# The folded query weight built in the output weight's room, two low parts of the value weight on GpSimd, and all queues in a new order

## The chip, the cores and the metric

The kernel runs on one core of a Trainium2 chip. A core has five instruction queues that run side by side and wait for one another by semaphores: TensorE (PE in the profile, its weight loads apart as PEld), VectorE (DVE), ScalarE (ACT), GpSimd (POOL) and SyncE (SP), which in this kernel issues all transfers. The metric is the device time of one execution in microseconds (us).

## The reference

Two layer types alternate, twice over, on 2048 rows of 512 numbers in float32. Both see the same weights each time.

```
x = x + A(layernorm(x))    # linear attention with a learned feature map
x = x + B(layernorm(x))    # relu(x @ w1) @ w2, inner width 1792
x = x + A(layernorm(x))
x = x + B(layernorm(x))

A(x): q, k, v = split(x @ wqkv)               # 32 heads of 16
      pq, pk = q @ w_phi, k @ w_phi           # per head
      phi = concat(softmax(p), softmax(-p))   # 32 features per head
      kv, z = sum_s phi_k v, sum_s phi_k
      o = (phi_q kv) / (phi_q z + 1e-6);  return o @ wo
```

Since `w_phi` follows `wqkv` with nothing between them, the kernel multiplies the key part and the query part of `wqkv` by `w_phi` once, at the start. It calls this folding.

## The kernel before

**Numbers in two halves.** Every float32 operand of a large product is scaled by a power of two and split into a float16 high part and a float16 low part, and a product is three matmuls: high by high, high by low, low by high (`PAIRS`, line 625). `split` (lines 417 to 431) makes the two parts of a weight: ScalarE writes the high part (line 419) and VectorE the low part as weight times scale minus high part (line 429). With `pool=True` ScalarE scales the weight in place as well and GpSimd subtracts (line 426).

**Tiles and stages.** The rows are taken in 16 blocks of 128 (`NCH`), in the feed-forward part in 8 tiles of 256 (`NT`). The front stage (lines 1635 to 1783) loads and prepares the weights and, block by block, normalises, makes keys and values (`keys`, `values`: 12 matmuls each, line 635) and sums them into a per-head table (`gather`). `opening` (line 1841) turns that table into a right-hand side, reads out the first queries, projects them with `wo` and normalises for the first feed-forward tile. Then `tile_steps` runs the feed-forward part, mixed with attention work of other blocks, and the whole is done once more for the second pair of layers.

**Folding.** `fold` (lines 1655 to 1706) takes a 512x512 weight in float32, `src`. For each of four column groups g, TensorE transposes four 128x128 blocks into a PSUM bank (line 1665, tile `wt_q`), and the bank is copied to SBUF (line 1670, tile `wT_q`). TensorE then multiplies the transposed weight by the block-diagonal `bd` made from `w_phi`, once for each of four row blocks k (line 1701, tile `pf_q`), and `split` makes the folded weight's parts `wq_h` and `wq_l` from that PSUM bank. The scale of the split comes from the sum of squares of the weight: ScalarE squares it (line 372, into the room of the low part as scratch), TensorE sums over partitions (line 382, tile `sb_q`), VectorE bounds it (line 387), GpSimd takes the power -1/2 (line 391), VectorE cuts it to a power of two (line 392). The four banks `wt_q` and the bank of `sb_q` and the four `pf_q` all come from the tag `h`, which has two banks: the third transposition needs the first copy done, the fourth the second copy, `sb_q` the third copy, the first `pf_q` the fourth.

**Rooms.** The 8 KB per partition pieces that hold a raw weight, or a transposed one, come from a pool with three rooms (`piece`, line 501). They are used by `st_k`, `st_v`, `wT_k`, `st_q`, `w1_last`, `wT_q`, `w2_last` and `wo_a`, made in this order; from the fourth on, each takes the room of one whose readers are done, and its first writer waits for the last of them. The parts of the folded and split weights have rooms of their own, four tiles of two (`Wq, Wk, Wv, Wo`, line 350). `Wo` is written by `wo_job` (line 1738), late in the front stage.

**What sets the order.** The program is a list of tasks with what each reads, writes and makes (`Plan.add`). `ORDER` (line 56) holds one string per queue; each digit says how many of the queue's remaining tasks, in the list's order, are passed over to find the next one (`Plan.queue`, line 213). The queues run in exactly that order, and each task waits for what it depends on. So a task that waits holds up all behind it in its queue.

The lines that the change touches:

Of the kernel before, what the change touches and what calls it, by code (L numbers as in the profile page):

```python
# [9 lines left out]
F32 = mybir.dt.float32  # L10
# [8 lines left out]
P = 128  # L19
# [35 lines left out]
DIGITS = "0123456789abcdefghijklmnopqrstuvwxyzABCDEFGHIJKLMNOPQRSTUVWXYZ"  # L55
ORDER = {
    PE:
        "000024222323210022000990837066622803359530620371010832920201713Q006310K3040G602E0810Az1y81420t0s0rr52061"
        "0m161i2hh0g30eh01fc0b0aaaaaaa01006605500001016050000105d0000000a00a4022001260000120304202030020214046621"
        "673005830133022111000001111006000000300000000000000000580000c00008e000gj00000000000000000000001111122222"  # L60
        "2222223022201111111222333333302222200000000011122011044a0e0000000000060000b00000111111110000000001110000"
        "000010300000000000000000500600c0bh00000000000b0000000000000011122222022222222222022222222222333444440333"
        "333333333334445555555577777788888999aa09008888899999999999aa09080060555044403333333302220000000000000000"
        "00000000111100100000011111122222022222222222333333333333337770666666055908888002240331100000060000006b00"
        "0000000000000001111111111000k0mjl001gg0f0e010b0aaaaagga090cddd010908077700504744403344361703111100330201"
        "1220666004450438000555044555aaaaaaaaaaaaaaaaaaabbbccccccccdddee0dd30b00990070055144033330201111111110000"
        "00001000000e0000000008000000008000000000d0G0000000000z0000000000I00000000000000000000000o00000000000l000"
        "000000000000000000e000000000000000t00000rK0000000000D0000000000000000000000p0000000000000000000000000000"
        "000800A000000000000000000l000000y00000000000000n00000000000000000000b00000000000000000000003000000000000"
        "000000f00000000a0000p0r000000000000000000000000b00000000000000000000003000000000000000000000000000000000"  # L70
        "00000000000000000000000000000000000000000000000000000000000000000000000000000000000000000000000000000000"
        "0000000000000000000000000000000003000",
    DVE:
        "33033020i110f333122132111gl16014039d042304b00h007300b00e0YdX0g00Te044e4d6f60I0c034c40A39j02h201h1g10000e"
        "j0dg77eh060e04130222220f1000440673001l10jk12h21f11111a112212117l162i21321b91a81pbo11a221pi00m22k20400000"
        "00001051706024363500570645045140883712201a0080700411311113001063500615660650368070404802001311a291171010"
        "0012245222002220110334402260500309081002420aa11006013131111312174004772066151006052000908556113122012226"
        "77167625772684706d1cc0i10ggg00e0011a119000607066337232043131200200022413080711117363107836a8837060060003"
        "502320062520330104400f4e100122116000004034030100000003360201200k0100g00000bb0091020c1b403300500hh0311d10"
        "11u51s00010v30tl232p252MM40aJ09OO20M076Za0Z904Z70400112223Z72000Z3133Zx10XZu1310Zq155f21310b11Zo1000cZj1"  # L80
        "009111ZJ1ZIZb071610ZB411ZI0441ZE101d1d10Zw1k002h36050402200292002520022520023f3010200082h300052422002521"
        "70250103221330322102a20082120e05322200620177022400200022211002200230005232200220022102210220021102120044"
        "2221020102200220301000010013100",
    ACT:
        "31201104220a02100ccbc5a30m07c7j0a150d202ai0h12mm4c2b5200Zq20jj0030Zim2l722Zc5g20ll37qq061e18c5411mm2020p"
        "4214l010Bn405k1000112051f2e112iGi01002ii0120u70100102m010u602012d31110iic800e9d6c907504499400600aa49020d"
        "db0g038100559g700440ia1083010a39050004635400051006006033494073601121033a308222502223011050030350300b1044"
        "4012000250120101174615b122021111030022061141033340100037111200020120620237201403903262340322201611130001"
        "1812a052103222014586705993074640445953830615908888447066bbc0fgb0f0ieh00ff0iie24f22a2bd2ca202806644a49447"
        "490577343308270325b51082226607565514660033325264003391088333026001300041061001100055200643021004043020gg"  # L90
        "0007102903100400e8800a6990510e531032203101460500f610c908900708074n06y6k650505e537m8lK4005G58U07C707Zq77M"
        "05K056Zh644544Zb0344Zn33001ZUZi44002Zd03111ZIj00030ZC22244401113f332ZD2130Zz2ZZa01002Zt2352030201000222Z"
        "NZZ50116055h0ZV10524457270050e020130201030Zd22260502310130330270055000524b031304003P30113022611022210504"
        "21021023321060524035103311704103301400206003022005042000002020000524030520322004040320400201030220030200"
        "00220000221140022004003321130220410220130220133010000",
    POOL:
        "10030574006a05079000960A06801v90046070b6008a00809e0070d0911180001010062522010a199407010445044130e0222208"
        "b0dfa0bcc080e7007250302000112100000220172151700506134021111310410000113022010350444300136134131200001100"
        "10440001706252112111700000020102b22288242043204030200000ddd11bb119c999a180807060413312033024440333004100"
        "1004102010000000000000011104030000066000001000010a09100020c0009cc0kk00tt007TT06001X10101S11Zj101Zgb33022"  # L100
        "222b022100Z9900Z60201101510020Zl4030232a40302211c2144130Z720121121O2112104030220330211120044406302204111"
        "m2011100024201333011311042336022250000000000002230133301111550444444423332222011100000331011111100000110",
    SP:
        "20001000201406086207z8b082a7b7cq8ud66eg055ef60151g255e44m171ao051g01e1g5121341077g004fl0h5d100it08210n44"
        "81g413h253200h0803057i3d3643n5401444408270007p050845ac62c3a340144g43e2016622649d1e45453b517al772514201bt"
        "662161956569bdq36337857651918401726aeg581dd125003b01a180a92c1cbc7a1a186a161w778a5681b0318884364d50v45q90"
        "86r1074j71025GF2t32B34c52e5k169200nu100za01c10a60808y24c0Cg50K913cb2090JbbSg8c84j98SZ447464m48947894l056"
        "714542Nb3120044002449652402a260511706301544142205751106622665012260511555141333041333000200",
}


# [164 lines left out]
def tile_kernel(ctx: ExitStack, tc: tile.TileContext, x_in, wqkv, w_phi, wo, w1, w2, out):  # L276
# [137 lines left out]
        src = inv if b is not None else a  # L414
        add(DVE, 0.15, lambda: nc.vector.reciprocal(inv.ap, src.ap), reads=[src], writes=[inv])

    def split(w, s, hi, lo, cols, reads, res, key, psum=False, pool=False):

        add(ACT, 0.16 + cols / 1160, lambda: nc.scalar.activation(hi(), w(), AF.Copy, scale=s.ap),
            reads=[*reads, s], writes=[(res, f"h{key}")])  # L420
# [8 lines left out]
        add(DVE, 0.12 + cols / 940, lambda: nc.vector.scalar_tensor_tensor(  # L429
            lo(), w(), s.ap, hi(), op0=ALU.mult, op1=ALU.subtract),  # L430
            reads=[*reads, s, (res, f"h{key}")], writes=[(res, f"l{key}")], lock=not psum)
# [1220 lines left out]
                   [(b, i if cuts > 1 else None)], [(W, f"l{k}") for k in range(KC)[ks]])  # L1652
        return sq

    def fold(src, W, name, t_banks, f_banks, copies, cuts=1):

        sq = squares_of(src, W, name, cuts)
        wT = piece(f"wT_{name}")
        pts = {}

        def blocks(i, g):
# [3 lines left out]
                nc.tensor.transpose(pts[g].ap[:, k * P:(k + 1) * P], f32_piece(src)[:, k, g * P:(g + 1) * P], ident)  # L1665

        def copy(g):
            if g == 0:
                wT.ap = wT.make()
            (nc.scalar.copy if copies[g] == ACT else nc.vector.tensor_copy)(f32_piece(wT)[:, g, :], pts[g].ap)  # L1670

        def turned(i, g, after=()):
            if i == 0:
# [3 lines left out]

        def copied(g):
            add(copies[g], 0.475 if copies[g] == ACT else 0.608, partial(copy, g), reads=[pts[g]],
                makes=[(wT, g)] if g == 0 else [], writes=[] if g == 0 else [(wT, g)])  # L1680

        if cuts > 1:
            for g in range(4):
# [11 lines left out]
        for k in range(KC):  # L1695
            pf = bank(f_banks[k], f"pf_{name}{k}")

            def products(k=k, pf=pf):
                pf.ap = pf.make()
                for g in range(4):  # L1700
                    nc.tensor.matmul(pf.ap[:, g * P:(g + 1) * P], f32_piece(wT)[:, g, k * P:(k + 1) * P],  # L1701
                                     bd.ap[:, g, :], start=True, stop=True)

            add(PE, 0.96, products, reads=[wT, bd], makes=[pf])
# [56 lines left out]
    for c in range(NCH):  # L1761
# [247 lines left out]
```

## Time and profile before

| | |
|---|---|
| three executions | 966.74, 967.08, 967.94 us; median 967.08 |
| the profiled execution | 966.96 us; span from first to last instruction 965.2 us |
| TensorE busy | 950.8 us of the span |
| VectorE, GpSimd, ScalarE busy | 694.2, 642.4, 571.1 us |
| granted TensorE clock | 1.000 |

The profile is one execution on the chip. A row of the timeline has the start, the duration, the engine, the line of the kernel, the operation, the tile written and the tiles read, the shape, and how many instructions the row joins; in square brackets the idle time of the engine before it, and what ended that. Matmuls are pipelined: one starts while the one before still runs, so the distance of the starts tells what a matmul costs TensorE. The windows view gives each engine's busy time in a stretch.

### The profile page before, as it was taken

What the parts mean: (1) busy time and instruction counts of PE and PEld (TensorE: products, weight loads), DVE (VectorE), ACT (ScalarE), POOL (GpSimd) and SP (SyncE); (2) the same over time, 40 slices, a digit from 0 to 9 for tenths busy, and PEclk for the clock granted to TensorE, in tenths of its full rate; (3) what the DMA queues carried; (4) which work ended last, traced back from release to release, by engine and by line L of the source; (5) the groups of instructions that cost most, each with busy time, mean ns of one, the idle gap of its engine ahead of it and who ended that gap; (6) DMA issues with size and microseconds to landing.
All of it is one profiled execution on the core that took longest, in us unless ns stands there. A gap on an engine that the chain in (4) does not pass through costs nothing.

```text
span 965.2 us, 24114 instructions
## 1 busy us (share of the span) xinstructions
PE 950.8 (99%) x9620; PEld 665.1 (69%) x9620; DVE 694.2 (72%) x1388; ACT 571.1 (59%) x1121; POOL 642.4 (67%) x630
## 2 busy tenths in 40 slices
PE   7999998999999999999999999999999999999998
PEld 5555554766565666667667875566667888898997
DVE  6889889974867768765485668987886665664454
ACT  7889978654454645455365564565546665555543
POOL 2598886678584866647367746268568787877563
PEclk9999999999999999999999999999999999999999
DMA  9367738577869587886938853799999886886542
GB/s 336 113 178 204 231 110 236 115 170 172 242 158 240 146 208 220 211 197 183 237 108 203 289 163 105 240 243 223 215 232 202 251 175 149 222 180 149 138 133 77
DMA packets 251809, 183.41 MB, mean 190 GB/s; under 512 B 180656, under 2 KB 188080, under 8 KB 251696
## 3 DMA queue, kind: packets, MB, share of 16 engines
q1 hardware_dynamic: 251696, 181.87, 72.3%
q8 instruction: 75, 1.23, 0.5%
q14 instruction: 38, 0.31, 0.1%
HBM read 108.30 MB, written 30.15 MB: 143 GB/s over the span
## 4 chain that ended last, share of the span: by engine, by line
PE 91%; DVE 4%; ACT 2%; DMA 1%; POOL 1%; issue 1%; SPq 0%; DVEq 0%; ACTq 0%; POOLq 0%
PE ph L1367 24%; PE py L1483 15%; PE py L1542 12%; PE pk L635 8%; PE pv L635 8%; PE pw L635 8%; PE pq L635 7%; PE ph L1447 4%; PE pn L953 2%; PE kv L803 2%; DMA xe<-in_A_x_dram 1%; DMA pT<-p_q 1%; POOL p_q L710 0%; DVE e_q L672 0%; PE pf_q L1701 0%
## 5 line engine op out<-in xcount | busy, mean ns | idle before, releaser
L1483 PE MATMUL py<-w,h 128*128 128x512 f16 x690 | 174.4, 379 | 0.0
L1367 PEld LDWEIGHTS <-s 128*128 128x128 f16 x2352 | 152.1, 98 | 30.8 <-issue 2.3
L1380 ACT ACTIVATE sn<-ph 128x128 f32<-128x128 f32 x294 | 80.3, 273 | 140.2 <-PE ph L1367 139.1
L635 PEld LDWEIGHTS <-xT 128*128 128x128 f16 x900 | 86.8, 98 | 98.8 <-issue 0.5
L1367 PEld LDWEIGHTS <-w 128*128 128x128 f16 x1764 | 111.1, 98 | 13.5 <-issue 0.2
L1367 PE MATMUL ph<-yT,s 128*128 128x128 f16 x1176 | 97.6, 219 | 1.4 <-DVE ph L1386 1.4
L1367 PE MATMUL ph<-yT,w 128*128 128x128 f16 x1176 | 97.6, 219 | 0.0
L1386 DVE TENSOR_TENSOR ph<-ph,sn 128x128 f32<-128x128 f32 x98 | 29.3, 299 | 92.9 <-PE ph L1367 54.0
L1483 PEld LDWEIGHTS <-h 128*128 128x128 f16 x690 | 61.4, 98 | 48.1
L699 POOL TENSOR_TENSOR e_q<-e_q,fm_q 128x1024 f32<-128x1024 f32 x32 | 64.0, 2000 | 39.6 <-ACT fm_q L695 39.5
L699 POOL TENSOR_TENSOR e_k<-e_k,fm_k 128x1024 f32<-128x1024 f32 x30 | 60.1, 2003 | 39.5 <-ACT fm_k L695 39.1
L710 POOL TENSOR_TENSOR p_q<-e_q,p_q 128x1024 f16<-128x1024 f32 x32 | 69.8, 2180 | 19.9 <-ACT p_q L706 19.8
L635 PE MATMUL pk<-wk_h,xT 128*128 128x512 f16 x256 | 81.3, 379 | 0.1
L635 PE MATMUL pv<-wv_h,xT 128*128 128x512 f16 x256 | 81.2, 379 | 0.0
L635 PE MATMUL pw<-wo_h,oT 128*128 128x512 f16 x256 | 81.2, 379 | 0.0
L710 POOL TENSOR_TENSOR p_k<-e_k,p_k 128x1024 f16<-128x1024 f32 x30 | 66.2, 2208 | 21.9 <-ACT p_k L706 21.6
L1391 DVE TENSOR_TENSOR ph<-ph,sn 128x256 f32<-128x256 f32 x98 | 41.9, 427 | 32.9 <-PE ph L1367 31.9
L635 PEld LDWEIGHTS <-oT 128*128 128x128 f16 x384 | 36.8, 98 | 40.2
L1542 PEld LDWEIGHTS <-h 128*128 128x128 f16 x648 | 59.2, 98 | 6.4
L1163 POOL TENSOR_TENSOR w<-r 128x256 f32<-128x256 f32 x41 | 32.2, 787 | 39.9 <-ACT r L1159 35.8
L635 PE MATMUL pq<-wq_h,xq 128*128 128x512 f16 x168 | 57.4, 379 | 0.0
L1159 ACT ACTIVATE r<-ph 128x512 f32<-128x512 f32 x54 | 32.0, 593 | 36.8 <-DVE ph L1391 36.5
(267 smaller groups left out, 2434.3 us busy)
## 6 DMA issues: line engine op xcount, KB each, us to landing
s<-s_dram SPq DMA_DIRECT2D x98, 512.0 KB, 4.5
q_dram<-qs SPq DMA_DIRECT2D x28, 256.0 KB, 2.9
ql<-q_dram SPq DMA_DIRECT2D x28, 256.0 KB, 3.7
u<-t_dram SPq DMA_DIRECT2D x13, 512.0 KB, 4.7
xt_dram<-xT SPq DMA_DIRECT2D x21, 256.0 KB, 4.8
xq<-xt_dram SPq DMA_DIRECT2D x21, 256.0 KB, 3.8
xe<-in_A_x_dram SPq DMA_DIRECT2D x16, 256.0 KB, 5.2
x<-in_A_x_dram SPq DMA_DIRECT2D x16, 256.0 KB, 3.9
```

What stands on the lines that cost most here:

```text
L635: nc.tensor.matmul(pm.ap, xT.ap[:, a, k, :], W.ap[b][:, k, :], start=(k == 0 and i == 0), stop=(k == KC - 1 and i == 2))
L699: (nc.vector if fast else nc.gpsimd).tensor_tensor(e3, e3, sm.unsqueeze(2).to_broadcast([P, 2 * n, DH]), op=ALU.mult)
L710: (nc.vector if fast else nc.gpsimd).tensor_sub(p16.ap[:, 1, cols], ef, p16.ap[:, 0, cols])
L1159: nc.scalar.activation(r.ap, ph.ap, AF.Relu)
L1163: nc.gpsimd.tensor_sub(rf.ap[:, :2, :], r.ap.rearrange("p (a b) -> p a b", a=4)[:, ::3, :], block(1).unsqueeze(1).to_broadcast([P, 2, P]))
L1367: nc.tensor.matmul(at(r), weight_of(i, b, kk, s, summed), rows_of(y, i, a, kk), start=(first and kk == 0 and n == 0), stop=(kk == 1 and n ...
L1380: nc.scalar.activation(saved(i), at(2), AF.Copy)
L1386: add(DVE, 0.27, lambda: nc.vector.tensor_tensor(at(3), at(1), saved(2), op=ALU.add), reads=[(ph, 1), (sn, 2)], writes=[(ph, 3)], boost=10 ...
L1391: add(DVE, 0.40, lambda: nc.vector.tensor_tensor(wide(ph), wide(ph), wide(sn), op=ALU.add), reads=[(sn, 0), (sn, 1)], writes=[(ph, 0), (ph ...
L1447: nc.tensor.matmul(at()[:, j, cs.start * P:cs.stop * P], W1.at(b, k, slice(f * P, (f + 1) * P)), yT.ap[:, cs, a, k, :], stop=(k == KC - 1 ...
L1483: nc.tensor.matmul(py.ap, h[a].ap.rearrange("p j t -> p (j t)")[:, cols], W2.at(b, fs[j], slice(0, D)), start=(begins and j == k == 0), st ...
L1542: nc.tensor.matmul(py.ap[:, 256 * r:256 * r + 256], left[a], right[b], start=(s == 0 and r == 0 and k == 0), stop=(last and k == 2), skip_ ...
```

## The change

Three things are changed.

1. `fold` can be given a `home`. For the query weight it is `Wo`: the transposed query weight is written, as float32, over the two part tiles of the output weight (two column groups in each), and no `piece` is made for it. The pieces are then seven: `st_k`, `st_v`, `wT_k`, `st_q`, `w1_last`, `w2_last`, `wo_a`.
2. `split` can be called with `aside`. For row blocks 2 and 3 of the value weight ScalarE makes the high part as before; GpSimd multiplies the raw weight by its scale in place and then subtracts the high part. VectorE's two instructions for these blocks go. The split of the value weight now marks the blocks of `st_v` one by one.
3. All five strings of `ORDER` are new.

```diff
-    def split(w, s, hi, lo, cols, reads, res, key, psum=False, pool=False):
+    def split(w, s, hi, lo, cols, reads, res, key, psum=False, pool=False, aside=False):
 
         add(ACT, 0.16 + cols / 1160, lambda: nc.scalar.activation(hi(), w(), AF.Copy, scale=s.ap),
             reads=[*reads, s], writes=[(res, f"h{key}")])
+        if aside:
+            add(POOL, 0.14 + cols / 700, lambda: nc.gpsimd.tensor_scalar(w(), w(), s.ap, None, op0=ALU.mult),
+                reads=[s], writes=reads)
+            add(POOL, 0.14 + cols / 523, lambda: nc.gpsimd.tensor_sub(lo(), w(), hi()),
+                reads=[*reads, (res, f"h{key}")], writes=[(res, f"l{key}")])
+            return
...
-    def fold(src, W, name, t_banks, f_banks, copies, cuts=1):
+    def fold(src, W, name, t_banks, f_banks, copies, cuts=1, home=None):
...
-        wT = piece(f"wT_{name}")
+        wT = piece(f"wT_{name}") if home is None else home
+        row = lambda g: f32_piece(wT)[:, g, :] if home is None else \
+            flat(home.ap[g // 2]).bitcast(F32)[:, g % 2 * 512:g % 2 * 512 + 512]
...
-            (nc.scalar.copy if copies[g] == ACT else nc.vector.tensor_copy)(f32_piece(wT)[:, g, :], pts[g].ap)
+            (nc.scalar.copy if copies[g] == ACT else nc.vector.tensor_copy)(row(g), pts[g].ap)
...
-                    nc.tensor.matmul(pf.ap[:, g * P:(g + 1) * P], f32_piece(wT)[:, g, k * P:(k + 1) * P],
+                    nc.tensor.matmul(pf.ap[:, g * P:(g + 1) * P], row(g)[:, k * P:(k + 1) * P],
...
     for k in range(KC):
         split(lambda k=k: f32_piece(st_v)[:, k, :], s_v, lambda k=k: Wv.ap[0][:, k, :],
-              lambda k=k: Wv.ap[1][:, k, :], 512, [st_v], Wv, k)
+              lambda k=k: Wv.ap[1][:, k, :], 512, [(st_v, k)], Wv, k, aside=k > 1)
...
-            fold(st_q, Wq, "q", "h" * 4, "h" * KC, (ACT,) * 4)
+            fold(st_q, Wq, "q", "h" * 4, "h" * KC, (ACT,) * 4, home=Wo)
```

The strings, read by the rule of line 213, give these queues in the stretch that the first two parts touch (k0 is the key product of block 0, x1 block 1 of the rows; "wT copy 0" is line 1670 for column group 0):

| queue | before | after |
|---|---|---|
| PE | sum v, wt_q 0, wt_q 1, **k0, wt_q 2**, x1 transposed, wt_q 3, **v0, sum q, pf_q 0, pf_q 1**, k1 | sum v, wt_q 0, wt_q 1, **wt_q 2, k0**, x1 transposed, wt_q 3, **sum q, pf_q 0, pf_q 1, v0**, k1 |
| ACT | wk_h 2, 3, 0, **x1 normalised, wk_h 1**, wv_h 2, 1, 0, 3, wT copy 0, 1, square of q, wT copy 3, x1 high, wT copy 2 | wk_h 2, 3, 0, **wk_h 1, x1 normalised**, wT copy 0, 1, wv_h 1, 3, 2, square of q, wT copy 2, 3, wv_h 0, x1 high |
| DVE | **statistics of x1, scale of k, x0 low**, wk_l 2, 3, 0, 1, **wv_l 2, 1, 0, 3**, k0 bounds, statistics of x2, x3 | **scale of k, x0 low, statistics of x1**, wk_l 2, 3, 0, 1, **wv_l 1**, k0 bounds, statistics of x2, bound of q, **wv_l 0** |
| POOL | power for v, for x2, x3, for q | power for v, **wv 3 multiplied, wv_l 3, wv 2 multiplied, wv_l 2**, for q, for x2, x3 |
| SP | x2, x3, w1 part 0, 2, x4, w1 part 1, x5, w1 last, x6 | x2, x3, x4, x5, w1 part 1, w1 last, w2 part 0, x6, w1 part 0 |

Over the whole program, counted among the tasks that both kernels have, 604 of 1493 tasks of PE stand at another place in their queue than before, 529 of 948 of DVE, 743 of 1071 of ACT, 347 of 618 of POOL and 426 of 506 of SP, in the mean by 0.8, 1.1, 1.6, 1.1 and 4.8 places.

More of the change, by code (lines that the diff above doesn't have):

```diff
@@ new lines @@
+    POOL:
+        "10070220044607009040960068070y016v0804607005908a0080900c700c911107001010062522010a194077a00074002022302b"
+        "22d0fh07md09ci00a008772034021103110400330017115100013633402111110111000014102220035504430013134112220000"
+        "111110033028070252222121151000020102222526455503050002010100ddd11bb1a199a9a18088000140222203302033333300"
+        "11201022300110000000000000201104030000066000001001000aa01000010b109cc0kk00tt91U0T7000411V020SZl0f000Zg41"
+        "302011c1020110Z99100Z50111000400Zn01030201219021121110238302220Z4210200N11100400201133301112155003302011"
+        "411n1011110002232033301411114130201121411211111000522244002111004444442333022111111111141444130222221000"
+        "0110",
@@ new lines @@
+    SP:
+        "2000100026912490c0egi0x8iaj450700542c33inan0342k808327v312161600314ec14b5c1a000279f10jg01120k81811q1b1j4"
+        "5314j24n323c2qa11471844d74a854915i13393v172822b787ce86e47b497772i62399552s8861a2df5674d2673864504g4117b7"
+        "12161957669b023a407717533380bb73833aegg3114c0041c1b34c48a220bcbc71080756013304544263248847740344459a99r0"
+        "a014p4135q6J3d3Gd535d00zn4141517x2d21g121x18bF711092a053b0Ba1d0Ic1cNbXe0jbpc6dc9V9a95575Z0nc14813697001U"
+        "145f24211100h4030352h4604412260003305526670132208551006622051322015141044444030244440200200",
@@ L1667, in copy @@
         def copy(g):
-            if g == 0:
+            if g == 0 and home is None:
                 wT.ap = wT.make()
-            (nc.scalar.copy if copies[g] == ACT else nc.vector.tensor_copy)(f32_piece(wT)[:, g, :], pts[g].ap)
+            (nc.scalar.copy if copies[g] == ACT else nc.vector.tensor_copy)(row(g), pts[g].ap)
         def turned(i, g, after=()):
@@ L1679, in copied @@
             add(copies[g], 0.475 if copies[g] == ACT else 0.608, partial(copy, g), reads=[pts[g]],
-                makes=[(wT, g)] if g == 0 else [], writes=[] if g == 0 else [(wT, g)])
+                makes=[(wT, g)] if g == 0 and home is None else [],
+                writes=[] if g == 0 and home is None else [(wT, g)])
         if cuts > 1:
```

81 lines of the change are left out of this document (35 added, 46 removed).

## The prediction

> **What bounds the kernel now.** I read the busy page first, then the chain that ended last, then the windows, then TensorE's waits, and the timeline only where TensorE stands still. The page:
>
> ```profile
> span 965.2 us, 24114 instructions
> PE 950.8 (99%) x9620; PEld 665.1 (69%) x9620; DVE 694.2 (72%) x1388; ACT 571.1 (59%) x1121; POOL 642.4 (67%) x630
> PEclk9999999999999999999999999999999999999999
> PE 91%; DVE 4%; ACT 2%; DMA 1%; POOL 1%; issue 1%; SPq 0%; DVEq 0%; ACTq 0%; POOLq 0%
> ```
>
> TensorE works 950.8 of 965.2 us at the full granted clock in every slice, and the chain that ended last is 91% its own. The change adds no matmul and removes none: it can only move the 965.2 - 950.8 = 14.4 us in which TensorE is idle. The windows view cuts the span where that idleness changes; its columns are the stretch and its length, then busy time of PE, PEld, DVE, ACT, POOL, clock, DMA share and GB/s:
>
> ```profile
> 0.00:26.31 26.31, 21.11 (x140) 15.75 (x141) 17.49 (x53) 19.89 (x32) 6.29 (x20) 1.00 0.93 340
> 26.31:153.00 126.69, 126.69 (x934) 65.93 (x932) 112.91 (x204) 112.08 (x170) 97.11 (x63) 1.00 0.59 168
> 153.00:168.05 15.05, 12.12 (x101) 6.60 (x100) 13.09 (x29) 11.96 (x17) 12.02 (x8) 1.00 0.80 230
> 168.05:952.00 783.95, 782.51 (x8373) 570.11 (x8372) 542.87 (x1091) 424.46 (x900) 524.00 (x538) 1.00 0.75 190
> 952.00:965.20 13.20, 8.40 (x79) 6.69 (x76) 7.87 (x15) 2.71 (x6) 2.96 (x4) 0.97 0.11 41
> ```
>
> The idle time is 5.20 us before the key product of block 1 (26.31), nothing in the rest of the front, 2.93 in the opening, 1.44 in 784 us of feed-forward work, and 4.80 in the end. The waits view names what it was for (total, times, longest):
>
> ```profile
> PE wt_q L1665 <- ACT wT_q L1670: 1.6, 1, 1.6
> PE ph L1367 <- DVE ph L1386: 1.4, 5, 0.5
> PE tr_b L578 <- ACT xn_b L612: 1.1, 1, 1.1
> PE pn L953 <- DMA pT<-p_q: 0.5, 1, 0.5
> PE tr_o L578 <- DVE dn L961: 0.4, 1, 0.4
> PE tr_o L578 <- DVE o L964: 0.3, 1, 0.3
> ```
>
> Only the first, 1.6 us, lies in the code that the first two parts of the change touch.
>
> **That stall.** Times in these rows: start, duration.
>
> ```profile
> 12.72 0.68 DVE L587 TENSOR_TENSOR xT<-tr_a,xT 128x512 f16<-128x512 f32 x1
> 12.89 1.84 ACT L419 ACTIVATE wk_h<-pf_k,s_k 128x512 f16<-128x512 f32 x3 [0.16 <-DVE s_k L402]
> 13.54 1.13 PE L1701 MATMUL pf_k<-bd,wT_k 128*128 128x128 f32 x8 [0.48 <-DVE stat_a L617]
> 14.62 0.82 ACT L612 ACTIVATE xn_a<-xe,stat_a 128x512 f32<-128x512 f32 x1
> 15.32 0.69 ACT L419 ACTIVATE wk_h<-pf_k,s_k 128x512 f16<-128x512 f32 x1
> 15.80 0.38 PE L635 MATMUL pk<-wk_h,xT 128*128 128x512 f16 x1
> 16.12 2.56 ACT L419 ACTIVATE wv_h<-st_v,s_v 128x512 f16<-128x512 f32 x4
> 16.88 2.74 DVE L429 SCALAR_TENSOR_TENSOR wv_l<-st_v,s_v,wv_h 128x512 f16<-128x512 f32 x4
> 18.36 0.38 PE L635 MATMUL pk<-wk_h,xT 128*128 128x512 f16 x1
> 19.71 1.07 ACT L1670 COPY wT_q<-wt_q 128x512 f32<-128x512 f32 x2 [1.02 <-DVE wv_l L429]
> 20.35 0.66 PE L1665 MATMUL wt_q<-ident,st_q 128*128 128x128 f32 x4 [1.61 <-ACT wT_q L1670]
> 20.67 1.92 ACT L372 ACTIVATE wq_l<-st_q 128x2048 bf16<-128x2048 f32 x1
> 20.84 0.60 PE L578 MATMUL tr_a<-ident,xn_a 128*128 128x128 f32 x4
> 21.28 0.60 PE L1665 MATMUL wt_q<-ident,st_q 128*128 128x128 f32 x4
> 21.71 0.38 PE L635 MATMUL pv<-wv_h,xT 128*128 128x512 f16 x1
> 24.30 0.28 PE L382 MATMUL sb_q<-sq_q,ones 128*128 128x1 f32 x2
> 24.44 2.03 PE L1701 MATMUL pf_q<-bd,wT_q 128*128 128x128 f32 x16
> 26.31 0.38 PE L635 MATMUL pk<-wk_h,xT 128*128 128x512 f16 x1
> ```
>
> VectorE's last low part of the value weight ends at 16.88 + 2.74 = 19.62, and the copy starts at 19.71: the transposed query weight was to be laid where the raw value weight still was. The copy held up the third transposition by 1.61.
>
> **Part 1, the new home.** That wait goes altogether: nobody has written or read `Wo` yet (`wo_job` comes late). No instruction is added. What is late next is ScalarE itself, by its new queue. Its squaring of the value weight holds it to about 12.66; the bound of the key's scale now stands before the statistics of x1 on VectorE, and so no longer comes later than that. By the spacing inside the rows above (three `wk_h` in 1.84 are 0.575 apart with a last one of 0.69; two copies in 1.07 are 0.48 apart with 0.58; four `wv_h` in 2.56 are 0.627 apart with 0.68) ScalarE then runs: `wk_h` 12.66, 13.24, 13.81, 14.39; x1 normalised 14.97 (0.70 of its 0.82 hold the next); copies 0 and 1 at 15.67 and 16.15, the first done at 16.25; `wv_h` 1, 3, 2 at 16.63, 17.26, 17.88; the square of q 18.51 (its 1.9 move with it); copies 2 and 3 at 20.41 and 20.89, done at 20.99 and 21.47; `wv_h` 0 at 21.37, done 22.05.
>
> TensorE, by the starts above: a group of four transpositions takes 0.43 to 0.49 (20.35, 20.84, 21.28, 21.71), 12 matmuls of a key or value product 2.59 (21.71 to 24.30), the sum 0.14, 16 folding matmuls 1.87 (24.44 to 26.31). Third transposition when copy 0 is out, 16.31; k0 16.80; x1 transposed 19.39; fourth 19.83; done 20.26. The sum of q wants the bank of copy 2 and waits to 21.03 (0.77); the first folding product wants that of copy 3, 21.51 (0.34); v0 23.38; **k1 at 25.97**, where it was 26.31. So the front gains 0.34 us, and not 1.61: before the third transposition TensorE now waits about 1 us for copy 0, and behind the fourth it waits 1.11 because the square stands ahead of copies 2 and 3. Against that go the 1.61, the 0.48 before the last folding product of the key (the low part of x0 moves ahead of x1's statistics, so its bank is free in time), and some 0.35 lost in and behind k0, which took 18.74 - 15.80 = 2.94 for work of 2.59. Bounds: if copies 2 and 3 were out in time, 1.11 more; if copy 0 came 0.7 later (x1 normalised waiting 0.7 for its load), 0.7 less, a loss of 0.36.
>
> **Part 2, two low parts on GpSimd.** VectorE loses two of four instructions of 2.74 (0.69 each, the spacing); nothing on the path waits for them, so this gives nothing by itself. GpSimd gets four: two subtractions and two multiplications. Nearest row for a two-input GpSimd operation on 128x512:
>
> ```profile
> 41.52 1.16 POOL L552 TENSOR_TENSOR n_a<-xn_a,n_a 128x512 f16<-128x512 f32 x1 [1.69 <-ACT n_a L549]
> 24.86 0.55 POOL L391 TENSOR_TENSOR m_q<-m_q,nhalf 128x1 f32<-128x1 f32 x1 [1.40 <-DVE inv_k L415]
> 147.34 1.22 DVE L672 TENSOR_TENSOR e_q<-ql,fm_q 128x1024 f32<-128x1024 f32 x1
> 152.73 2.00 POOL L699 TENSOR_TENSOR e_q<-e_q,fm_q 128x1024 f32<-128x1024 f32 x1 [1.58 <-ACT fm_q L695]
> 152.85 2.96 DVE L672 TENSOR_TENSOR e_q<-ql,fm_q 128x1024 f32<-128x1024 f32 x1
> ```
>
> A subtraction costs 1.16. The multiplication by a per-partition scale (T) is in no trace: between 0.55, a column of one element, and, upward, the 2.00 of an operation on twice the elements. I take 1.16, the row of the same shape. The chain starts when `wv_h` 3 is out, about 18.0, and ends at 18.0 + 2.32 + 2T = 20.32 + 2T: 22.6. TensorE wants it in the value product's third row block, 23.38 + 7 x 0.216 = 24.9, so by itself it is covered up to T = 2.2. Behind it in GpSimd's queue stand the power for q, wanted when the sum of q is out (21.2), and the powers for x2 and x3, 0.55 each: they slip to about 24.3 at the latest, where before the power for q ran at 24.86. Nothing there is lost.
>
> The dearer question is the last two rows: the same VectorE instruction took 1.22 alone and 2.96 beside GpSimd's; it seems to have stood until GpSimd was done at 154.73 and then run its 1.1. `wv_l` 0 on VectorE reads two tiles in SBUF as well. If it may not start while GpSimd's chain runs, it ends at 20.32 + 2T + 0.75 = 23.4 at T = 1.16, and v0 wants it at 23.6, its second matmul: just covered. Beyond T = 1.27 every 0.1 costs 0.2 us.
>
> The Trainium skill, in "SBUF — State Buffer", section "Who interferes with whom", says that a VectorE instruction with two SBUF inputs contends with a GpSimd instruction that reads SBUF, and that whoever issued first holds the shared pair for its whole instruction while the other blocks. The pair of rows agrees (2.96 against 1.22). By that rule VectorE could slip in between two GpSimd instructions, and `wv_l` 0 would end earlier than 23.4; without any lock it would end at 22.8. By all three the sum here is the same at T = 1.16, and differs only above 1.27.
>
> **Part 3, the order.** No transfer is added or removed. In the rest of the front TensorE has no idle time, and followed through the queues to the key product of block 4 near 50 us nothing is late: the 0.34 is carried. SP takes x4 and x5 ahead of the parts of `w1`; the first use of a `w1` part is far beyond that, and `w1_last` still finds the room of `wT_k` free. The later pieces lose nothing by one piece fewer. In the opening ScalarE's reciprocals' copy (line 695) goes behind line 422, so GpSimd's 2.00 starts some 1.1 later, after VectorE's 1.22 instead of on it: the numerators come about 1.5 earlier, and the two waits of 0.4 and 0.3 at `tr_o` may go, while `xn_b`, which follows a power on GpSimd, moves by only 0.3. I book 0, bounds -0.7 (both gone) and +1.3 (GpSimd's 2.00 ahead of that power, and both gone). In the feed-forward part there are 1.44 us to win, at most; new waits are the open side, each like the existing ones (0.46 and less). I book 0, bounds -0.5 and +2.5. In the end two row steps change places on TensorE, VectorE's queue is the same: 0.
>
> **Sum.** The profiled execution took 966.96 (its span and 1.76 around it), 0.12 below the median of 967.08. 966.96 - 0.34 = 966.62; put to the median, 966.7.
>
> **Rivals.**
> Emptied stall: copies 2 and 3 don't delay TensorE, since the square runs early. For it: ScalarE is free to 12.66 only by the squaring of v, and each row I moved could be 0.1 off. Against: the square has 1.9 us and stands ahead of them by queue. Gain 0.34 + 1.11 = 1.45, 965.6; with the 0.7 in the opening, 964.9.
> GpSimd as the bound: T is large and `wv_l` 0 waits for its chain. Price 2T - 2.53 above T = 1.27; it eats the 0.34 at T = 1.44, and passes 0.2% at T = 2.4. At T = 2.5 it costs 2.5: 969.2. For it: 2.96 beside 1.22. Against: no row of that size takes more than 1.16.
> New waits in the feed-forward stretch: 743 ScalarE tasks and 426 transfers stand elsewhere, TensorE's cover there is 782.51 of 783.95, so any move can only lose. Five waits of 0.46 are 2.3, ten 4.6: 969 to 971. Against: moves are of about one place on four queues.
> No effect: gaps of the old size appear elsewhere, 967.1.
>
> **How the numbers follow.** My forecast with its own range of 966.0 to 967.6 (the 1.11 not quite won, or a wait or two): 0.50. No effect 0.10. Emptied stall 0.16. GpSimd as the bound 0.06. New waits 0.18. 0.2% is 1.9 us, about what a measurement of this kernel can tell from no change: 965.1 and 969.0. Below 965.1 needs the emptied stall and the opening's part: 0.13. Above 969.0: most of the new waits and half of the GpSimd case, 0.19. Range 964.9, the best case worked out, to 969.8, which takes in the GpSimd case and the milder half of the waits.
>
> **What would show it.** Right: the third transposition waits for copy 0 alone, no VectorE low part in ScalarE's waits; two gaps near 21 us at `sb_q` and `pf_q`; k1 at about 26.0; GpSimd rows of 1.16 near 18 to 22.6; idle time of 5, 0, 3, 1.5 and 4.8 in the same windows. Wrong: GpSimd rows over 1.3 for the multiplication and a gap at v0; a wait of TensorE between 26 and 153; more than five `ph` waits; an opening off by more than 0.7.

## The result and the profile after

The changed kernel takes 973.18 us (median of six, 970.72 to 974.09), the kernel before 967.97 in its six: a ratio of 1.0043, with a 95% interval of 1.0030 to 1.0056. By the ratio it is slower by about 4 us (2.9 to 5.4). I had forecast 966.7 with a range to 969.8: wrong. The profiled execution of the changed kernel took 973.75, its span is 972.0 (before: 966.96 and 965.2). The two profiles are 6.8 us apart, more than the ratio says: that of before is one of its fastest executions, that of the changed kernel one of its slower ones. One execution of one later version (the exchanged VectorE instructions) took 1100.54 us at a granted clock of 0.85 and is left out of that version's median.

The page and the windows view of the changed kernel. The stretches are cut at the same points of the work as those shown of before: the key product of block 1, the opening, the feed-forward work, the end.

```profile
span 972.0 us, 24127 instructions
PE 953.4 (98%) x9620; PEld 666.5 (69%) x9620; DVE 691.6 (71%) x1386; ACT 572.9 (59%) x1121; POOL 653.0 (67%) x634
PE 86%; DMA 4%; POOL 3%; DVE 3%; ACT 3%; issue 1%; SPq 0%; DVEq 0%; POOLq 0%; ACTq 0%
```
```profile
0.00:25.57 25.57, 21.50 (x141) 16.06 (x142) 15.92 (x50) 19.37 (x31) 11.31 (x23) 1.00 0.94 343
25.57:153.00 127.43, 127.43 (x937) 66.28 (x936) 113.88 (x204) 113.24 (x171) 96.80 (x63) 1.00 0.61 172
153.00:166.40 13.40, 11.07 (x98) 6.24 (x97) 11.27 (x29) 11.09 (x16) 11.35 (x8) 0.98 0.59 150
166.40:958.80 792.40, 784.99 (x8372) 571.17 (x8372) 542.41 (x1091) 426.34 (x901) 530.49 (x538) 1.00 0.75 189
958.80:972.00 13.20, 8.42 (x79) 6.73 (x76) 8.08 (x15) 2.83 (x6) 3.03 (x4) 0.98 0.11 41
```

In the first line of stretches block 1 begins at 25.57, where it was 26.31; the opening has 2.33 us of idle TensorE for 2.93. The loss is in the fourth line: 7.41 us idle of 792.40, where it was 1.44 of 783.95. Transfers (DMA) are now 4% of the chain that ended last; they were 1%. Some of TensorE's waits:

```profile
PE ph L1374 <- DVE ph L1393: 2.1, 4, 1.1
PE pk L642 <- DMA xT<-n_a: 1.4, 1, 1.4
PE ph L1374 <- DVE h L1105: 1.2, 1, 1.2
PE tr_b L585 <- ACT xn_b L619: 1.2, 1, 1.2
PE pn L960 <- DMA pT<-p_q: 1.0, 1, 1.0
PE pw L642 <- DMA oT<-n_o: 1.0, 2, 0.5
PE wt_q L1674 <- ACT wo_h L1679: 0.7, 1, 0.7
PE ph L1374 <- DMA s<-s_dram: 0.6, 1, 0.6
```

The 1.6 us wait for the copy is gone. In its place stand five waits for transfers (`oT` twice, `s`, `pT`, `xT`) and two of over 1 us for VectorE. To see what each costs, I set the start of the same matmul in the two traces side by side:

| after this wait (time in the changed kernel) | the same matmul is later than before by | step |
|---|---|---|
| key product of block 1, 25.6 | -0.74 | -0.74 |
| first `tr_b`, 164.3 | -1.65 | -0.91 |
| a stretch at half clock, 165 to 170 | -0.41 | +1.24 |
| `pw` for `oT`, 184 and 219, idle 0.46 and 0.54 | +0.94 | +1.35 |
| `ph` for `s`, 300, idle 0.58 | +1.80 | +0.86 |
| `pn` for `pT`, 347, idle 1.00 | +2.98 | +1.18 |
| `pk` for `xT`, 409, idle 1.44 | +4.58 | +1.60 |
| `ph` for VectorE's `h`, 462, idle 1.22 | +5.97 | +1.39 |
| smaller waits, 500 to 508 | +6.24 | +0.27 |
| `ph` for VectorE's `ph`, 535, idle 1.05 | +7.46 | +1.22 |
| end (a wait of before near 635 does not come) | +6.81 | -0.65 |

Each wait costs some 0.16 us more than its idle time, because the last matmul ahead of it runs out uncovered: a matmul takes 0.379 us, but the next one starts 0.216 us after it when nothing holds it up. In this execution 5.0 us go to transfers that land late, 2.6 to the two waits for VectorE, 0.27 to smaller ones and 1.24 to the clock.

### The profile page after: what moved, and what is told of

Read it like the earlier page. It is cut to its first block, busy times and chain, and to the rows that moved or that the text cites. A ratio compares the mean times of both kernels' runs of the same rounds, so it can differ in the third digit from the quotient of the medians.

```text
span 972.0 us, 24127 instructions
## 1 busy us (share of the span) xinstructions
PE 953.4 (98%) x9620; PEld 666.5 (69%) x9620; DVE 691.6 (71%) x1386; ACT 572.9 (59%) x1121; POOL 653.0 (67%) x634
## 3 DMA queue, kind: packets, MB, share of 16 engines
q8 instruction: 75, 1.23, 0.6%
## 4 chain that ended last, share of the span: by engine, by line
PE 86%; DMA 4%; POOL 3%; DVE 3%; ACT 3%; issue 1%; SPq 0%; DVEq 0%; POOLq 0%; ACTq 0%
PE ph L1374 22%; PE py L1490 13%; PE py L1549 11%; PE pv L642 8%; PE pq L642 8%; PE pk L642 8%; PE pw L642 7%; PE ph L1454 3%; PE pn L960 2%; PE kv L810 2%; DMA oT<-n_o 1%; DMA st_v<-in_A_wqkv_dram 1%; DMA pT<-p_q 1%; DMA s<-s_dram 1%; DMA xT<-n_a 1%
## 5 line engine op out<-in xcount | busy, mean ns | idle before, releaser
L1102 ACT ACTIVATE h<-ph 128x512 f16<-128x512 f32 x58 | 34.2, 590 | 35.7 <-DVE ph L1398 23.6
```

Of the source, the lines that this page charges most:

```text
L1102: nc.scalar.activation(h[0].ap, at(), AF.Relu)
```

## The experiments

The theory after this reading (A): the first two parts and the opening's order gain 1.65 us, and the new order of the feed-forward work loses all the rest. The rival (B): it is the first two parts that lose, since the feed-forward work meets its transfers at another time. Task lists of both kernels were cut at 166.5 us, and the queues joined crosswise.

**The changed front, the old rest.**

```diff
 ORDER, each queue of the changed kernel:
-    all tasks in the new order
+    tasks that start before 166.5 us in the kernel before: in the new order; all others: in the order of before
```

> The changed kernel up to 166.5 us (all three parts of the change), and behind it each queue in the order of before. Theory A, the loss is made by the new order of the feed-forward work: this one keeps the gain of the front and the opening (key product of block 1 at 25.6, first tr_b at 164.3 instead of 166.0) and no more than 1.5 us of waits from 168 to the end; 965.2 to 965.7, about 1.6 below before. Theory B, the loss comes of the first two parts, because the feed-forward work then meets its transfers at another time: waits of 5 us and more appear as in the changed kernel, 970 or above.

966.18 us against 968.34 of before in the same job, ratio 0.9977 (0.9966 to 0.9987). First `tr_b` comes 0.91 earlier against the key product of block 1 than before (165.19 - 26.42 = 138.77; before 165.99 - 26.31 = 139.68). This version beats both kernels. Its windows view, the feed-forward part:

```profile
168.00:952.00 784.00, 781.77 (x8366) 569.57 (x8364) 542.19 (x1091) 424.60 (x900) 524.03 (x537) 1.00 0.75 191
```

784.00 - 781.77 = 2.2 us idle, more than the 1.5 expected, of which 1.03 is a wait for `pT` at 345. That is far from the 5 us and more of theory B: theory A holds, B falls.

**The old front, the changed rest.**

```diff
 ORDER, each queue of the kernel before:
-    all tasks in the old order
+    tasks that start before 166.5 us: in the old order; all others: in the changed kernel's order
```

> The kernel before (old home, no GpSimd low parts) in its own order up to 166.5 us, and the changed kernel's order of all queues behind it. Theory A: no gain ahead, and some 6 us of waits behind, 972 to 974. Theory B: as before, 966.5 to 968.

974.68 us, ratio 1.0064 (1.0049 to 1.0079). The waits are the changed kernel's, one by one:

```profile
PE pk L635 <- DMA xT<-n_a: 1.4, 1, 1.4
PE pn L953 <- DMA pT<-p_q: 1.2, 1, 1.2
PE ph L1367 <- DVE h L1098: 1.2, 1, 1.2
PE pw L635 <- DMA oT<-n_o: 1.0, 2, 0.5
```

So they do not need the new home or GpSimd. Those for `oT` (184 and 219), `xT` and VectorE hang on the order: they stand in the profiles of the changed kernel and of this version, and at these places in no profile with the old rest. The one for `pT` does not: versions with the old rest have it too (1.03, 1.06 and 1.21 in three of them), and one with the new rest lacks it: the one with exchanged VectorE instructions, whose queues up to that point are those of the changed kernel. So its 1.18 in the table cannot be charged to the new order. The profiled execution of this version had no stretch at half clock, so the loss does not come of the clock either.

**Only the transfers' queue in the new order.**

```diff
 ORDER, the kernel before:
-    SP: old order
+    SP: from 166.5 us in the changed kernel's order; PE, DVE, ACT, POOL: old order
```

> The kernel before with only the queue that issues the transfers (SP) in the changed kernel's order behind 166.5 us; the four engines keep their order. If the new waits of theory A come of the transfers' order alone: 3 us or more of waits on transfers (oT, xT, pT, s), 970 to 973. If they come of the engines' order: as before, 966.5 to 968.

1001.34 us, ratio 1.0338. TensorE waits 15.5 us for `s` in five waits. This told little: transfers in one order and engines in another hold each other up, far beyond the changed kernel's loss. No run has the reverse (new engines, old SP queue), so which queue carries the loss stays open. I looked at the single waits instead.

**The new home alone.**

```diff
+    fold(st_q, Wq, "q", "h" * 4, "h" * KC, (ACT,) * 4, home=Wo)      # the kernel before, all queues as before
```

> The kernel before with the new home for the transposed query weight alone; every queue as before. The copies wait for ScalarE's own fourth high part (ends 18.68) and no longer for VectorE's low part (19.62): third transposition 1.0 earlier, key product of block 1 at 25.3, 966.0. By the rival that ScalarE's order takes the gain back: 26.0, 966.7.

The mechanism came as expected, the third transposition at 19.37 after a wait of 0.47, the key product of block 1 at 25.33:

```profile
18.75 1.04 ACT L1672 COPY wo_h<-wt_q 128x512 f32<-128x512 f32 x2
19.37 0.66 PE L1667 MATMUL wt_q<-ident,st_q 128*128 128x128 f32 x4 [0.47 <-ACT wo_h L1672]
```

The time did not: 968.15 against 968.34, ratio 1.0000 (0.9984 to 1.0016). In the profiled execution the 0.98 is more than given back (its span is 967.4, that of before 965.2), by a stretch at half clock behind the opening (granted 0.72 from 165 to 170 us) and by two waits for transfers, `pT` 1.06 at 345 and `oT` 0.79 at 713. A gain of 1 us is not visible in this kernel's time while such waits come and go.

**No low part on GpSimd.**

```diff
     (the kernel with the changed front and the old rest)
-              ..., Wv, k, aside=k > 1)
+              ..., Wv, k)
+    VectorE's queue: low parts of blocks 3 and 2 right behind that of block 1
```

> The kernel with the changed front and the old order behind, but with all four low parts of the value weight on VectorE again (blocks 3 and 2 right behind block 1). If the GpSimd low parts give nothing: the same as with them, 966 to 967, and key product of block 1 within 0.2 of it. If they carry the front's gain: 0.5 or more later.

966.71, ratio 0.9979 (0.9968 to 0.9991), beside 966.18 and 0.9977 with them. From the first folding product of the key to the key product of block 1 it takes 25.89 - 10.04 = 15.85 us, and 26.42 - 10.66 = 15.76 with them. So the second part of the change gives and costs nothing that these runs can show.

**The home's gain and the opening's together.**

```diff
 ORDER, the kernel before with the new home:
-    all tasks in the old order
+    tasks that start from 130 to 166.5 us: in the changed kernel's order; all others: old order
```

> The new home alone in the front (all queues in the order of before up to 130 us), the changed kernel's order from there through the opening (130 to 166.5 us), the order of before behind it; no low part on GpSimd. If the two gains add, 1.1 in the front and 0.9 in the opening: about 2.0 below before and 0.7 below the kernel with the changed front. If the opening's gain hangs on the changed front: 1.1 below before.

967.83, ratio 0.9989 (0.9979 to 0.9999). The join at 130 us opens waits of its own, 0.94, 0.10 and 0.26 for ScalarE's `v` from 144 to 148 us, which take the opening's gain. Inconclusive on whether the two gains add.

**VectorE beside GpSimd.** The rows of the changed kernel at the two waits for VectorE:

```profile
457.99 2.13 POOL L717 TENSOR_TENSOR p_q<-e_q,p_q 128x1024 f16<-128x1024 f32 x1 [1.17 <-ACT p_q L713]
458.08 3.13 DVE L679 TENSOR_TENSOR e_q<-ql,fm_q 128x1024 f32<-128x1024 f32 x1
461.13 0.68 DVE L1105 SCALAR_TENSOR_TENSOR h<-ph,h 128x512 f16<-128x512 f32 x1
...
532.17 2.08 POOL L706 TENSOR_TENSOR e_k<-e_k,fm_k 128x1024 f32<-128x1024 f32 x1 [0.99 <-ACT fm_k L702]
532.39 2.28 DVE L1195 TENSOR_TENSOR w<-fold,w 128x384 f16<-128x384 f32 x1
534.59 0.29 DVE L1393 TENSOR_TENSOR ph<-ph,sn 128x128 f32<-128x128 f32 x1
534.93 0.27 PE L1374 MATMUL ph<-yT,s 128*128 128x128 f16 x2 [1.05 <-DVE ph L1393]
```

The numerators took 3.13 where 1.22 is usual, and line 1195 took 2.28 for 0.56 (its neighbour at 531.31 has that). Each began just behind a GpSimd instruction of 2.1 us that reads two tiles, ended 1.09 and 0.42 behind it, somewhat less than its usual duration, and the instruction that TensorE waited for stood next in VectorE's queue.

```diff
 ORDER, DVE of the changed kernel:
-    ..., e_q (line 679), h (line 1105), ...          near 461 us
+    ..., h (line 1105), e_q (line 679), ...
-    ..., w (line 1195), ph (line 1393), ...          near 534 us
+    ..., ph (line 1393), w (line 1195), ...
```

> The changed kernel with two pairs of neighbours exchanged in VectorE's queue, so that the instruction TensorE waits for stands ahead of the one that stretches beside GpSimd: activation of the hidden part (line 1105) ahead of the query numerators (line 679) near 461 us, the sum of line 1393 ahead of line 1195 near 534 us. If the stretched VectorE instructions make these two waits: 1.2 and 1.05 gone, 2.3 below the changed kernel, about 971. If something else is late there too: the waits stay, 973.

969.99, ratio 1.0017 (1.0005 to 1.0030), where the changed kernel has 1.0043 (1.0030 to 1.0056): 0.26%, 2.5 us. That this is nearly the 2.3 expected is in part luck. Set side by side with the changed kernel's trace, the two exchanges gain 0.59 and 1.21 us, 1.80 together; the wait for `pT`, worth 1.18, is also gone, and the edit does not touch it. VectorE's rows at the same places:

```profile
460.52 0.69 DVE L1105 SCALAR_TENSOR_TENSOR h<-ph,h 128x512 f16<-128x512 f32 x1 [1.03 <-ACT h L1102]
461.13 1.40 DVE L679 TENSOR_TENSOR e_q<-ql,fm_q 128x1024 f32<-128x1024 f32 x1
...
534.06 0.30 DVE L1393 TENSOR_TENSOR ph<-ph,sn 128x128 f32<-128x128 f32 x1 [0.86 <-PE ph L1374]
534.27 1.14 DVE L1195 TENSOR_TENSOR w<-fold,w 128x384 f16<-128x384 f32 x1
```

Both waits are gone. The instructions behind them still stretch (1.40 and 1.14), but TensorE no longer waits for them. Half of the first wait comes back as a wait of 0.64 at 463, where line 1393 now stands behind VectorE's statistics of a block.

**The late transfers.** The three transposing transfers for `oT` (179.12, landed 184.00; 214.58, landed 219.40) and `xT` (403.95, landed 409.25) took 4.88, 4.82 and 5.30 us, while nothing issued earlier was still on its way. Such a transfer usually takes 3.06. The one for `pT` took 6.26. What the four have in common is found in the DMA view: a packet of the instruction queue q8. Here is the changed kernel from 403.95 to 409.25; the first two rows are the busy share and GB/s in 40 slices.

```profile
DMA  0000000006999998007049996000000000299919
GB/s 0 0 0 0 0 0 0 0 14 145 211 263 201 147 50 17 8 8 131 8 89 263 278 286 2 0 0 0 4 8 10 8 10 12 64 426 402 340 46 448
...
q8 instruction: 1, 0.02, 1.6%
q14 instruction: 1, 0.01, 0.4%
```

The transposition runs at 145 to 263 GB/s, breaks off half way, goes on, and then nearly nothing moves for over a microsecond although loads are waiting. The q8 packet starts at 406.39. On the whole page q8 has 75 packets and 1.23 MB, so 16.4 KB each; TensorE's queue has 9620 + 9620 instructions, 256.5 for each packet, and in this trace the packets come 191 to 332 of TensorE's instructions apart, 255 in the median. I take it that they bring TensorE's code. The Trainium skill, "Runtime: NRT & Kernel Launch", section "Instruction fetch mechanics", says that an engine's instructions are refilled in blocks of 16 KiB, 256 instructions, through a DMA queue; the count agrees. It also calls the cost of such a block mostly hidden; for TensorE's own queue nothing here speaks against that. Where a fetch falls among the transfers depends on how many instructions TensorE has issued by then, so 120 instructions more at the start (60 matmuls with their weight loads; the expectations say 64) should move each by about half a period:

```diff
-            for _ in range(4):
-                nc.tensor.matmul(warm.ap[:, :256], ones.bitcast(F16)[:, :P], ones.bitcast(F16), start=True, stop=True)
+            for _ in range(16):
+                nc.tensor.matmul(warm.ap[:, :64], ones.bitcast(F16)[:, :P], ones.bitcast(F16)[:, :64], start=True, stop=True)
```

> The changed kernel with 64 narrow warming matmuls more at the start (80 of 64 columns in place of 20 of 256), so that TensorE's code, which is fetched about every 256 of its instructions, is fetched some 6 us earlier against the work. If the fetches make the four late transfers (near 184, 219, 347 and 409 us): those land after 3 to 4.5 us and the waits of 0.5, 0.5, 1.0 and 1.4 go, about 3 below the changed kernel, unless fetches fall on others. If the neighbouring transfers make them late: the same waits at the same places, 973.

971.73, ratio 1.0032 (1.0021 to 1.0044), where the changed kernel has 1.0043 (1.0030 to 1.0056): 1 us less, and the intervals overlap, so the times do not show the gain of 3 that was expected. The traces do show what happens to the waits. In this one all five waits for transfers between 184 and 409 us are gone. The same transposition, with the same transfers behind it at the same distances, and its DMA view from 401.07 to 404.5:

```profile
401.07 1.23 SPq L570 DMA_TRANSPOSE xT<-n_a  x1
402.41 0.55 SPq L1253 DMA_DIRECT2D seconds<-in_B_w_dram  x1
403.02 0.48 SPq L1332 DMA_DIRECT2D s<-s_dram  x1
...
404.82 0.38 PE L642 MATMUL pk<-wk_h,xT 128*128 128x512 f16 x1
```
```profile
DMA  0000000000000099999999940010999999000139
GB/s 0 0 0 0 0 0 0 0 0 0 0 0 0 21 221 197 212 203 191 218 185 122 57 21 9 6 9 12 224 287 287 287 290 288 24 0 0 48 119 310
...
q14 instruction: 1, 0.01, 1.0%
```

No q8 packet, and the transfer landed after 3.41 us instead of 5.30; those for `oT` after 3.09 and 3.06. The break half way is there without a packet too; what is gone is the microsecond of near standstill behind it. At 404.82 this kernel is 4.48 ahead of the changed one. Further on it gives some back and ends 3.3 ahead: other transfers are now met, `xT` at 514 (0.28), `oT` at 652 (0.70), `xq` at 678 (0.30). The two VectorE waits, 1.22 and 1.06, stay.

So the neighbouring transfers alone do not make these landings late. But the fetch alone does not either: in the kernel before, a packet fell on the same first `oT` transfer at the same place, 2.70 us after its issue (changed: 2.73), and it landed after 3.05. First before (178.3 to 181.5), then changed (179 to 184):

```profile
q8 instruction: 1, 0.02, 2.4%
oT<-n_o SPq DMA_TRANSPOSE x1, 3.1
```
```profile
q8 instruction: 1, 0.02, 1.2%
...
q_dram<-qs SPq DMA_DIRECT2D x2, 256.0 KB, 4.2
...
oT<-n_o SPq DMA_TRANSPOSE x1, 4.9
```

In before nothing was issued behind it until it landed; in the changed kernel five transfers were. It is the same with the second `oT` (packets 2.84 and 2.81 us after the issue; one transfer behind it and 3.05, five and 4.82). The `xT` transfer had its neighbours in before as well, but no packet, and landed after 3.06. So the late landings of `oT` and `xT` take both, a fetch in the transfer's time and several transfers issued behind it. The new order brought the second to `oT` and the first to `xT`. By what way the two together hold a transfer up, no run shows.

**Both edits.** The exchanges in VectorE's queue and the 60 matmuls.

> The changed kernel with both edits: the two exchanges in VectorE's queue and the 64 warming matmuls more. If the late transfers and the stretched VectorE instructions are the whole of the loss, nothing but some 2 us of waits is left from 168 us to the end, and the gain of the front and the opening shows: 967, at or below the kernel before. If there is a third cause: 970 or more.

969.33, ratio 1.0012 (1.0000 to 1.0024); idle TensorE 13.8 us in all, as little as before (14.4). No wait from 168 us on is longer than 0.63. That is 0.31% better than the changed kernel, but 2 us more than I expected, and not below before: the gain of the front and the opening does not show. Its trace, beside that of before, shows why: a half-clock stretch behind the opening takes 1.2 to 1.4, and five small waits that before has not (0.36, 0.43, 0.40, 0.63 and 0.19, from 281 to 652 us) take 2.0, and their tails 0.8, while before's wait near 635 is gone. So the two edits do not remove the whole of what the new order costs.

**The same shift in the kernel before.** The diff of the code shift, applied to the kernel before.

> The kernel before with the 64 warming matmuls more and nothing else. If they act only by where the code is fetched: other transfers are met, within 1.5 us of the kernel before in either direction, 967 to 970. If the narrow matmuls themselves help (a better start): 1 us or more below it and an earlier key product of block 1.

973.04 us, ratio 1.0050 (1.0031 to 1.0069), slower than either expectation. Waits open where before had none or shorter ones: `s` at 393 (0.41), `pT` at 637 (0.73), `sn` at 826 (0.38), `oT` at 834 (0.65); and the half-clock stretch stands behind the opening. In the trace, which ends 4.4 later than that of before, the stretch takes 1.4 and the waits and their tails the rest. The 60 matmuls change nothing in the order, so the order of before, too, was good only with the start that it had. That it is the fetches that open these waits is likely by the section on the late transfers, but was not looked into for each of them.

## Why the prediction was wrong

**The front was right.** I had the key product of block 1 at 25.97, 0.34 earlier. It came at 25.57, and 0.31 of the difference is that the first folding product of the key started at 9.84 instead of 10.15 (the kernels run here had it between 9.4 and 10.7, by the landing of the first weight). From that product on the gain is 16.16 - 15.73 = 0.43. The steps are those of the hand chain:

```profile
15.91 0.66 PE L1674 MATMUL wt_q<-ident,st_q 128*128 128x128 f32 x4 [0.68 <-ACT wo_h L1679]
17.67 1.57 POOL L423 TENSOR_SCALAR st_v<-st_v,s_v 128x512 f32<-128x512 f32 x1 [2.46 <-ACT wv_h L420]
18.06 1.92 ACT L373 ACTIVATE wq_l<-st_q 128x2048 bf16<-128x2048 f32 x1
19.96 1.08 ACT L1679 COPY wo_l<-wt_q 128x512 f32<-128x512 f32 x2
20.47 1.56 POOL L423 TENSOR_SCALAR st_v<-st_v,s_v 128x512 f32<-128x512 f32 x1
20.60 0.38 PE L383 MATMUL sb_q<-sq_q,ones 128*128 128x1 f32 x2 [0.57 <-ACT wo_l L1679]
21.69 0.75 DVE L436 SCALAR_TENSOR_TENSOR wv_l<-st_v,s_v,wv_h 128x512 f16<-128x512 f32 x1
22.11 1.34 POOL L425 TENSOR_TENSOR wv_l<-st_v,wv_h 128x512 f16<-128x512 f32 x1
```

A first wait of 0.68 for copy 0 (I had about 1), a second of 0.57 at `sb_q` behind the square (I had 0.77), a third of 0.10 at the folding product (I had 0.34). The new home alone, with the old queues, gains 0.98, or 1.13 from the first folding product on (16.16 - 15.03): the new order of the queues takes more than half of it back.

**GpSimd's price was too low, and harmless.** The multiplication took 1.57, not the 1.16 that I took. By my sum for a VectorE instruction that must wait for GpSimd's whole chain that would have cost 2 x 1.57 - 2.53 = 0.6. It cost nothing: `wv_l` of block 0 started at 21.69, in the middle of a multiplication that ran from 20.47 to 22.03, and took 0.75, its usual time (so in the four other traces with these instructions, 0.74 or 0.75). The subtraction that followed took 1.34 for 1.16. Here a multiplication by a scale, with one tile to read, did not hold VectorE up; a GpSimd instruction with two tiles did (3.13 for 1.22). The Trainium skill's rule in "SBUF — State Buffer", "Who interferes with whom", that VectorE with two SBUF inputs contends with any GpSimd instruction that reads SBUF, agrees with the second and not with the first; the trace decides.

**The opening was under-booked.** I wrote 0 with a bound of -0.7. Both waits at `tr_o` went, as described, and with their tails that is 0.91.

**The step that failed** is this one: "In the feed-forward part there are 1.44 us to win, at most; new waits are the open side, each like the existing ones (0.46 and less). I book 0, bounds -0.5 and +2.5." In the profiled execution it cost 7.9 us of new waits and their tails (5.0 of transfers, 2.6 of VectorE, 0.3 of smaller ones), less 0.65 for one of before that went; 1.18 of it, the wait for `pT`, may be chance. Two things are wrong in it. A new wait need not be like an old one: those that stood in the trace were what an order with little idle time had left over, and say nothing of what one moved task can open. The sizes were to be read elsewhere in the same trace: the 2.96 for a VectorE instruction beside GpSimd was quoted, but asked about in the front only, though GpSimd is busy for 524 of the 784 us of the feed-forward part. The second cause, transfers that a code fetch and the transfers issued behind them hold up, was in no term of the sum; the q8 row stood on the page of before (75 packets), and the landings of its transposing transfers scattered from 2.7 to 8.0 us (median 4.3). The rival "New waits in the feed-forward stretch" named the direction and 969 to 971. Its argument was the right one, but it got a chance of 0.18 only, and its "against", that tasks move by about one place, does not protect: a transfer that moves by one place can come to stand right behind a transposition.

## What to carry to other kernels

Where the bounding engine is busy for 99.8% of a stretch, a new order of that stretch has next to nothing to win, and each move can lose: price it by the scatter of what it moves (here landings of 2.7 to 8.0 us, an instruction of 1.2 to 3.1 us), not by the waits that are left. Keep a gain in one stage apart from the rest: the changed front with the old order behind it is the fastest kernel here, at 0.9977 of before (0.9979 with all low parts on VectorE). And a difference of 4 us in a thousand need not come of the order itself: 60 small matmuls at the start, which move the code fetches, made the order of before slower by 5 us, while the changed one became 1 us faster, within the noise.

## What was not expected of the hardware

**Code fetches and transfers.** Taken over the twelve traces, before and changed kernel included: transposing transfers of the short kind (all but `pT`), issued when nothing issued earlier was still on its way. Where no instruction packet was under way in their first 3.06 us, 126 landed after a median of 3.06 us, none after more than 3.79. Where one started 1.6 to 3.06 us after the issue, it depended on what was issued behind them within 3.0 us: with at most two transfers, 11 of 12 landed within 3.29; with three or more, 14 of 17 took 4.52 to 5.30. Where the packet started earlier, they took 3.05 to 4.36 (30).

**Half clock behind the opening.** The windows view of the changed kernel:

```profile
160.00:165.00 5.00, 3.80 (x19) 1.71 (x18) 4.03 (x10) 3.52 (x5) 4.38 (x4) 1.00 0.50 114
165.00:170.00 5.00, 3.87 (x38) 3.73 (x38) 3.39 (x7) 3.19 (x5) 4.75 (x5) 0.66 0.78 149
```

The granted clock is 0.66 over 5 us, that is half for 3.4 us, behind waits of 1.20, 0.69 and 0.45. It cost 1.24. The kernel before has much the same waits there (1.11, 0.69, 0.45) and a clock of 1.00 in its profile, and the kernel with the new home alone, whose queues are those of before, has 0.72: it comes in some executions and not in others. Two of the six executions of the changed kernel had a granted clock of 1.000, and took 971.79 and 970.72. The Trainium skill, "TensorE: Matmul & The Clock Gate", "Part 1: The HAM clock gate (the "warmup" mystery)", says that activity is judged in free-running windows of some 3.4 us; the length agrees. By that rule it would depend on where the gaps fall in a window, which no run here shows.
